# Streaming attention heads: own key tile and preceding block in place of a split window and a separate sink product

## The chip, the cores and the metric

The kernel runs on one core of a Trainium2 chip. The core has TensorE (PE in the profile, with its weight loads as PEld), VectorE (DVE), ScalarE (ACT), GpSimd (POOL) and SyncE (SP), which run their own instruction streams and meet at semaphores. The metric is the time of one execution on the device in microseconds (us). The kernel before takes 270.92 us, the median of three runs from 270.86 to 271.66.

## What is computed

Attention over 4 batches, 8 heads, 768 positions and a head size of 64, then a gated feed-forward layer on the 3072 x 512 result. Heads 0, 2 and 6 are retrieval heads and see all earlier positions. Heads 1, 3, 4, 5 and 7 are streaming heads: a query sees the first 4 positions (the sinks) and the last 64 (the window).

```python
rel = pos[:, None] - pos[None, :]
causal = rel >= 0
stream_keep = causal & ((pos[None, :] < 4) | (rel < 64))
scores = where(causal if retrieval[h] else stream_keep, q @ k.T / 8, -1e9)
x = softmax(scores) @ v                       # heads joined: 3072 x 512
g, val = x @ w_gate, x @ w_val                # 512 -> 1536
ffn = (gelu(g) * val) @ w_out                 # 1536 -> 512
out = x + sigmoid(x @ w_res) * ffn
```

## The kernel before

The work is cut into 24 query tiles of 128 rows, four to a chunk, six chunks (chunk 0 does its attention in two halves of two tiles). Heads go in pairs: (0,2), (4,6), (1,3), (5,7). Python builds a graph of tasks with priorities, and a scheduler orders each engine's tasks; `HINTS` replaces the priorities of single tasks by number. It lets the attention of the next chunk run between the feed-forward matmuls of the current one. All matrices are float16, PSUM is float32.

PE's array is used in four ways, and the scheduler knows them as modes: whole (128 rows x 128 columns), "row" (two halves of 64 rows, for the scores of two heads at once), "col" (two halves of 64 output rows) and "quarter" (four groups of 32 output rows).

For a streaming head, keys lie transposed in `qkt` (features in partitions). A query tile of 128 is scored in two halves of 64 queries, each against the 128 keys that end where it ends:

```python
# scores(), line 857, mode "row"; kt is None for a streaming head
parts = [(max(0, q0 * 128 - 64 + 64 * s), q0 * 128 + 64 * s, 64, o + 64 * s) for s in range(2)]
...
e.matmul(at(scr)[:, oo:oo + w], lhsT=side(BB, low, 1)[half, k0:k0 + 128],
         rhs=side(BB, low, 0)[half, qq:qq + w], start=True, stop=True)
```

The exp (ACT, line 873) moves them to SBUF, and a mask is multiplied on (DVE, line 909). Then the weights times values, with v and a copy `vs` of v that is shifted by 64 rows. Each half of 64 queries is a matmul on half of the array, two at a time:

```python
# weigh() / windows(), line 981, mode "col"; 0.03 us planned for each pair
for s in range(2):
    val = at(BB.v)[:, i, h, :] if s or i == 0 else at(BB.vs)[:, i - 1, h, :]
    r.append(e.matmul(at(av)[64 * s:64 * s + 64, o:o + 65],
                      lhsT=at(P.et)[:, w + 64 * s:w + 64 * s + 64], rhs=val, ...))
```

The sinks are a product of their own. One block a chunk (two in chunk 0) scores all five streaming heads against 32 keys on quarters of the array, one exp follows (`ek`), and each head and tile with a preceding tile adds one whole-array matmul with `vk`, a tile that is zero but for the sink rows:

```python
# sink_scores(), line 948, mode "quarter"
e.matmul(at(scr)[32 * j:32 * j + 32, o:o + w_], lhsT=at(BB.qkt)[half, 1, p, 0:32], rhs=..., ...)
# sinkf(), line 1005, whole array
e.matmul(at(av)[:, o:o + 65], lhsT=at(sinks.et)[:, ko:ko + 128], rhs=at(batch(b).vk)[:, sl, :], ...)
```

Retrieval heads take one whole-array matmul for each key tile (line 991). The other lines that the prediction names: 679 transposes q and k for chunks 0 and 1, 694 empties these to `qkt`; 1116 (and 1098 for halves of chunk 0) are the gate and value matmuls, 1128 the gelu; 1146 is the residual gate, 1161 the second feed-forward product; 1178 are matmuls on a blank tile that keep PE busy until the first gate matmul; 603 fills `vk`, 622 copies to `vs` in chunk 0.

```python
# PSUM banks by kind: (how many at once, which)
"sc": (2, [(2, 3), (4, 5)]), "gv": (4, one(6, 7, 5, 4, 3, 2)), "av2": (1, [(0, 1)]), "out": (2, one(6, 7))
```

Of the kernel before, what the change touches and what calls it, by code (L numbers as in the profile page):

```python
# [4 lines left out]
NHEAD = 8  # L5
SEQ = 768
# [36 lines left out]
VK = ((1, 4), (3, 4), (4, 5), (4, 7))  # L43
# [3 lines left out]
    "0:-96.05 3:-32.5 13:-14.98 398:-205.14 399:-3161.01 400:-242.48 401:-60.67 406:194.11 428:585.68 "  # L47
    "430:523.84 442:461.16 444:1172.07 587:-105.78 592:-108.69 613:396.07 617:407.42 620:-11.7 640:556.2 "
    "642:106.88 643:194.09 646:-2979.21 649:-102.44 659:511.02 686:-2.88 687:77.5 695:496.52 696:499.45 "
    "698:-3129.77 703:60.14 704:-184.95 705:-133.38 707:183.02 708:380.49 711:7.46 712:149.85 713:-50.64 "  # L50
    "715:-14.97 722:1121.95 725:480.98 726:449.69 731:-39.24 732:60.67 733:-318.24 737:-43.72 738:419.39 "
    "739:143.85 743:67.93 744:-230.75 746:-318.2 749:428.99 755:137.07 756:5.66 757:60.69 761:-9.34 "
    "762:495.92 764:2489.99 778:1098.32 789:2479.4 791:2501.2 807:953.41 837:1156.8 842:1419.06 877:2567.99 "
    "879:1563.79 880:2429.98 883:2507.13 898:1013.73 933:1964.55 937:1029.47 939:1471.24 940:2476.14 "
    "955:3421 962:3506.26 963:3575.25 971:3584.03 984:2490.73 989:3565.66 1020:3589.17 1022:2520.47 "
    "1036:2494.69 1066:3486.98 1103:3422.44 1109:3530.5 1114:4315.61 1115:4410.02 1124:-926.78 1134:4596.47 "
    "1141:3465.41 1143:2510.98 1146:2495.35 1152:4653.43 1157:112.2 1170:3039.97 1193:107.93 1248:3488.54 "
    "1265:3479.95 1266:4395.47 1271:4430.01 1272:4484.04 1275:-26.92 1284:5420.01 1289:3472.11 1290:4444.38 "
    "1293:-34.14 1295:3453.61 1302:4490.78 1305:3510.02 1316:3998.02 1318:3550.85 1319:3550.87 1320:4107.35 "
    "1349:3529.55 1351:5429.99 1355:3583.42 1414:5485.04 1451:1066.16 1462:4552.31 1474:4473.03 1475:6343.89 "  # L60
    "1480:4497.31 1530:6505.9 1534:2349.36 1556:5501.98 1602:6498.99 1637:6513.87 1670:7448.62 1687:7406.44 "
    "1689:5504.27 "
# [120 lines left out]
VK_AT = -18.5  # L183
VS_DMA = 0
# [277 lines left out]
def build_kernel(nc, q, k, v, w_gate, w_val, w_out, w_res, out):  # L462
# [7 lines left out]
    m_win = sb("m_win", [128, 7, 128], FP16)  # L470
# [9 lines left out]
    P_vs = Pool(many("vs", 2, [128, NT - 1, NHEAD, DHEAD + 1], FP16))  # L480
    P_vk = Pool(many("vk", 2, [128, 8, DHEAD + 1], FP16))
    P_qkt = Pool(many("qkt", 2, [128, 2, NPAIR, SEQ], FP16))
    P_q6 = Pool(many("q6", 2, [128, 2, SEQ], FP16))
    P_er = Pool(many("er", 2, [128, 4608], FP16))
    P_es = Pool(many("es", 2, [128, 1024], FP16))
    P_ek = Pool(many("ek", 1, [128, 640], FP16))
# [29 lines left out]
    def chain(prio, fns):  # L516
        prev = None
        for n, fn in fns:
            prev = G.add("pool", c_pool(n), fn, [prev], prio, name="const")
        return prev  # L520

    def spread(on, prio, dst, src, n, dep):
        return G.flex({e: (0.15 + 0.0003 * n if e == "dve" else 0.45, lambda e_, e=e: (
            e_.activation(out=dst, in_=src, func=AF.Copy) if e == "act" else e_.tensor_copy(out=dst, in_=src)))
            for e in on}, [dep], prio, name="spread")
# [5 lines left out]
    t_causal = chain(-54, [(128, lambda e: e.memset(m_causal[:, :], 1.0)),  # L531
                           (128, aff(m_causal[:, :], ALU.is_ge, 0.0, 0, [[1, 128]], -1))])


    t_win = chain(-53, [
        (256, lambda e: e.memset(m_win[:, 1:3, :], 1.0)),
        (256, aff(m_win[:, 1:3, :], ALU.is_ge, 0.0, -1, [[0, 2], [0, 2], [-1, 64]], 1)),
        (256, aff(m_win[:, 1:3, :], ALU.is_ge, 0.0, WINDOW, [[0, 2], [0, 2], [1, 64]], -1)),

        (64, aff(m_win[:, 2, 64:128], ALU.is_ge, 1.0, -N_SINK, [[0, 64]], 1)),  # L540
        (64, lambda e: e.memset(m_win[:, 2, 0:64], 1.0)),
        (64, aff(m_win[:, 2, 0:64], ALU.is_ge, 0.0, 0, [[1, 64]], -1))])
    t_win0 = [spread(("dve",), -50, m_win[:, 3:5, :], m_win[:, 1:2, :].to_broadcast([128, 2, 128]), 256, t_win)]

    t_win = t_win0 + [spread(("dve",), 600, m_win[:, 5:7, :], m_win[:, 1:2, :].to_broadcast([128, 2, 128]), 256, t_win),
                      spread(("dve",), 600, m_win[:, 0, :], m_win[:, 1, :], 128, t_win)]
    for i, vk in enumerate(P_vk.items):
        P_vk.last[i] = [G.add("dve", 0.5, (lambda vk=vk: lambda e: e.memset(vk[:, :, :], 0.0))(), [t_blank], -94, name="vzero")]
# [31 lines left out]
    def batch(b):  # L580
        if b not in batches:
            B_ = B()
            B_.v, B_.vs, B_.vk, B_.qkt = Buf(P_v), Buf(P_vs), Buf(P_vk), Buf(P_qkt)
            B_.vtok, B_.vstok, B_.qtok, B_.ktok = {}, {}, {}, {}

            B_.q6, B_.q6tok = None, {}
            batches[b] = B_
        return batches[b]

    def values(b, a, z, base, each, on_engines=False):  # L590
# [6 lines left out]
        if a == 0:  # L597

            def vk(on, j, h0, h1):
                def fn(e):  # L600
                    o = at(BB.vk)[32 * j:32 * j + N_SINK, 2 * j:2 * j + 2, :]
                    i_ = at(BB.v)[0:N_SINK, 0, h0:h1 + 1:h1 - h0, :]
                    return e.activation(out=o, in_=i_, func=AF.Copy) if on == "act" else e.tensor_copy(out=o, in_=i_)
                return fn
            BB.vktok = [G.flex({"dve": (0.3, vk("dve", j, *hs)), "act": (0.35, vk("act", j, *hs))},
                               [BB.vtok[0]], base + 1500, bufs=[BB.v, BB.vk], name="vk") for j, hs in enumerate(VK)]
            for t in BB.vktok:
                t.slack = 12.0 if b else 0.0
                if b == 0:

                    t.eng, t.alts, t.prio = "pool", None, VK_AT
                    t.dur, t.deps = 0.3, t.deps + [x for x in G.tasks if x.name == "const"]
        a_ = max(a, 1)
        if on_engines:
            ts = []
            for lo, hi, pr in ((1, 2, -75),) + (() if VS_DMA else ((2, 4, 130),)):
                for dst, src, off in ((0, 64, 1), (64, 0, 0)):
                    def vs(on, dst=dst, src=src, off=off, lo=lo, hi=hi):
                        def fn(e):
                            o = at(BB.vs)[dst:dst + 64, lo - 1:hi - 1, :, :].rearrange("p i h d -> p (i h d)")  # L620
                            i_ = at(BB.v)[src:src + 64, lo - off:hi - off, :, :].rearrange("p i h d -> p (i h d)")
                            return e.activation(out=o, in_=i_, func=AF.Copy) if on == "act" else e.tensor_copy(out=o, in_=i_)
                        return fn
                    n_ = (hi - lo) * 520
                    ts.append(G.flex({"dve": (c_dve(n_, 2.4, False), vs("dve")), "act": (c_act(n_), vs("act"))},
                                     [BB.vtok[i - off] for i in range(lo, hi)], pr, bufs=[BB.v, BB.vs], name="vs"))
# [651 lines left out]
```

The softmax here doesn't subtract the row's maximum and nothing guards it: scores larger than these inputs give would overflow.

## Time and profile before

| | us |
|---|---|
| time, median of three | 270.92 |
| span of the profiled execution | 268.8 |
| DVE busy / ACT busy / POOL busy | 140.1 / 139.9 / 87.3 |
| gate and value matmuls of 512 columns (line 1116, two groups) | 74.3 + 74.1 |
| second feed-forward product (line 1161) | 70.4 |
| scores (line 857, biggest group) | 16.9 |
| sink products (line 1005), 100 matmuls | 6.6 |
| window products (line 981), 240 matmuls in four groups | 5.7 + 5.5 + 2.1 + 2.0 |

The granted TensorE clock is 1.000 throughout. A busy time of PE counts each matmul from its start to its modelled end, merged where they overlap, so mean durations (379 ns for 512 columns) are longer than the distance between starts. The page also has a chain of work that ended last, waits by engine, a timeline of instructions and busy times in chosen windows; the lines that carry the reading stand in the prediction.

### The profile page before, as it was taken

To read this page: it belongs to the slowest core of one execution; us is meant where nothing else is said; L and a number is where in the kernel's file an instruction comes from. 1 tells how busy PE (TensorE), PEld (TensorE's weight loads), DVE (VectorE), ACT (ScalarE), POOL (GpSimd) and SP (SyncE) were. 2 spreads that over 40 slices of the span, in tenths; PEclk is the share of its full clock that TensorE was granted. 3 is DMA by queue.
4 is the path that set the end of the run, shared out by engine and by line. 5 is a ranking of instruction groups with operands and counts; after the bars stand their busy time and mean duration, and the time that the engine had idled before them with its cause. 6 is when DMAs were issued, how large, how long until landed. Compare 5 with 4: busy or idle time off the path is not lost.

```text
span 268.8 us, 5676 instructions
## 1 busy us (share of the span) xinstructions
PE 264.2 (98%) x2391; PEld 138.7 (52%) x2391; DVE 140.1 (52%) x273; ACT 139.9 (52%) x215; POOL 87.3 (32%) x124
## 2 busy tenths in 40 slices
PE   8999999999999999999999999999999999999995
PEld 7677465465444455444455444555444455444444
DVE  2698245485264376445476433486145367534344
ACT  3785358783334877136792243984233788233310
POOL 8999508995808029894000000000000000000000
DMA  6999999999999999999994100022000113200013
GB/s 86 171 205 207 185 180 228 169 168 187 171 129 187 154 160 185 216 189 125 184 148 134 41 0 0 2 41 96 25 0 0 39 41 80 78 2 0 1 39 120
DMA packets 97562, 29.38 MB, mean 109 GB/s; under 512 B 85504, under 2 KB 93952, under 8 KB 97536
## 3 DMA queue, kind: packets, MB, share of 16 engines
q0 software_dynamic: 70320, 14.69, 65.5%
q1 hardware_dynamic: 27216, 14.33, 27.9%
q8 instruction: 19, 0.31, 0.5%
q14 instruction: 7, 0.06, 0.1%
HBM read 29.36 MB, written 6.29 MB: 133 GB/s over the span
## 4 chain that ended last, share of the span: by engine, by line
PE 93%; DMA 3%; POOL 1%; DVE 1%; issue 0%; POOLq 0%; DVEq 0%
PE ps L1116 44%; PE ps L1161 23%; PE ps L1146 8%; PE ps L857 5%; PE ps L991 3%; DMA va<-in_v_dram 3%; PE ps L1098 3%; PE ps L981 2%; PE ps L1005 2%; PE ps L1070 1%; POOL qks L555 1%; PE ps L948 1%; PE ps L679 1%; PE ps L1178 1%; DVE otile L1168 0%; DVE otile L1165 0%
## 5 line engine op out<-in xcount | busy, mean ns | idle before, releaser
L1130 DVE SCALAR_TENSOR_TENSOR hT<-gact,ps 128x512 f16<-128x512 f16 x68 | 45.8, 686 | 67.4 <-ACT gact L1128 36.6
L1128 ACT ACTIVATE gact<-ps 128x512 f16<-128x512 f32 x68 | 40.1, 597 | 74.0 <-PE ps L1116 72.5
L1116 PE MATMUL ps<-xT,wv 128*128 128x512 f16 x272 | 74.3, 379 | 0.0
L1116 PE MATMUL ps<-xT,wg 128*128 128x512 f16 x272 | 74.1, 379 | 0.0
L1161 PE MATMUL ps<-wo,hT 128*128 128x512 f16 (+2 forms) x312 | 70.4, 363 | 0.0
L1116 PEld LDWEIGHTS ps<-xT,wg 128*128 128x128 f16 x272 | 26.3, 98 | 31.5 <-ACT xT L1077 0.6
L1116 PEld LDWEIGHTS ps<-xT,wv 128*128 128x128 f16 x272 | 26.2, 98 | 30.5 <-DVE hT L1130 0.5
L1161 PEld LDWEIGHTS ps<-wo,hT 128*128 128x128 f16 x312 | 27.5, 98 | 27.0 <-issue 0.7
L873 ACT ACTIVATE er<-ps 128x1024 f16<-128x1024 f32 (+4 forms) x40 | 34.2, 891 | 9.5 <-PE ps L857 9.4
L555 POOL DMA_DIRECT2D qks<-in_k_dram x36 | 28.3, 827 | 32.4 <-DMA qkt<-qks 21.9
L555 POOL DMA_DIRECT2D qks<-in_q_dram x36 | 28.8, 840 | 0.8 <-POOLq L1260 0.8
L1165 DVE SCALAR_TENSOR_TENSOR otile<-srs,ps 128x512 f32<-128x512 f32 (+2 forms) x26 | 16.8, 644 | 16.5 <-PE ps L1161 16.4
L1146 PE MATMUL ps<-wr,xT 128*128 128x512 f16 x96 | 24.7, 379 | 0.0
L555 POOL DMA_DIRECT2D va<-in_v_dram x24 | 21.6, 926 | 2.7 <-PE ps L1005 2.7
L1149 ACT ACTIVATE srs<-ps 128x512 f32<-128x512 f32 x24 | 14.3, 597 | 15.6 <-PE ps L1146 15.3
L1048 DVE TENSOR_TENSOR xtok<-ps,rcp 128x512 f32<-128x512 f32 (+1 forms) x28 | 16.9, 609 | 0.6
L1168 DVE TENSOR_TENSOR otile<-otile,xtok 128x512 f32<-128x512 f32 (+2 forms) x26 | 16.8, 647 | 0.7
L857 PE MATMUL ps<-qkt 64*128 64x64 f16 (+4 forms) x391 | 16.9, 213 | 0.0
L857 PEld LDWEIGHTS ps<-qkt 64*128 64x128 f16 x391 | 9.8, 94 | 9.4 <-issue 3.4
L873 ACT ACTIVATE es<-ps 128x1024 f16<-128x1024 f32 (+1 forms) x14 | 12.6, 898 | 2.9 <-PE ps L857 2.6
L1146 PEld LDWEIGHTS ps<-wr,xT 128*128 128x128 f16 x96 | 8.7, 98 | 10.0 <-issue 0.7
L1178 PE MATMUL ps<-blank 128*128 128x128 f16 x116 | 11.4, 249 | 1.1 <-DVE blank L527 1.1
(70 smaller groups left out, 212.5 us busy)
## 6 DMA issues: line engine op xcount, KB each, us to landing
out_dram<-otile SPq DMA_DIRECT2D x23, 256.0 KB, 2.2
va<-in_v_dram POOLq DMA_DIRECT2D x24, 128.0 KB, 17.0
qks<-in_k_dram POOLq DMA_DIRECT2D x32, 64.0 KB, 11.9
qks<-in_q_dram POOLq DMA_DIRECT2D x32, 64.0 KB, 12.4
wg<-in_moe_w_gate_dram POOLq DMA_DIRECT2D x3, 512.0 KB, 10.3
wv<-in_moe_w_val_dram POOLq DMA_DIRECT2D x3, 512.0 KB, 10.6
wo<-in_moe_w_out_dram POOLq DMA_DIRECT2D x4, 384.0 KB, 22.2
vs<-va SPq DMA_DIRECT2D x4, 260.0 KB, 7.4
```

Of the source, the lines that this page charges most:

```text
L555: return G.add(eng, issue, lambda e: e.dma_start(out_ap(), in_ap), deps, prio, bufs=bufs, dma=cost, name=name, grp=grp)
L857: return [e.matmul(at(scr)[:, oo:oo + w], lhsT=side(BB, low, 1)[half, k0:k0 + 128], rhs=side(BB, low, 0)[half, qq:qq + w], start=True, sto ...
L873: return e.activation(out=o, in_=i_, func=AF.Exp, scale=SM_SCALE)
L1048: t2 = G.add("dve", c_dve(2 * n * 64), lambda e: e.tensor_tensor(out=xview(), in0=avv(0, DHEAD), in1=scale(), op=ALU.mult), [t1] + xdeps, ...
L1116: return lambda e: [e.matmul(at(dst)[:, :], lhsT=w[:, ci, f * 128:(f + 1) * 128], rhs=at(xtbuf)[:, ci, :], start=(ci == 0), stop=(ci == NC ...
L1128: ta = G.add("act", c_act(512), (lambda gb=gb, ga=ga: lambda e: e.activation(out=at(ga)[:, :], in_=at(gb)[:, :], func=AF.Gelu))(), [tg], p ...
L1130: th = G.add("dve", c_dve(512), (lambda vb=vb, ga=ga, f=f: lambda e: e.scalar_tensor_tensor(out=at(h)[:, f, :], in0=at(ga)[:, :], scalar=0 ...
L1146: e.matmul(at(rb)[:, :], lhsT=at(xtbuf)[:, ci, s], rhs=wr[:, ci, :], start=(ci == 0), stop=(ci == NCB - 1))
L1149: ta = G.add("act", c_act(512), (lambda rb=rb, sr=sr: lambda e: e.activation(out=at(sr)[:, :], in_=at(rb)[:, :], func=AF.Tanh, scale=0.5)) ...
L1161: e.matmul(at(fb)[:, w], lhsT=at(h)[:, fi, s], rhs=wo[:, fi, w], start=(fi == 0), stop=(fi == NF - 1))
L1165: t1 = G.add("dve", c_dve(n), (lambda fb=fb, sr=sr, ot=ot, w=w: lambda e: e.scalar_tensor_tensor(out=at(ot)[:, w], in0=at(sr)[:, w], scala ...
L1168: t2 = G.add("dve", c_dve(n), (lambda ot=ot, lt=lt, w=w: lambda e: e.tensor_tensor(out=at(ot)[:, w], in0=at(ot)[:, w], in1=at(xbuf)[:, lt, ...
```

## The change

Each streaming head now handles a query tile as a retrieval head would: the tile against its own 128 keys, one 128-column score matmul and one whole-array product. The keys before it come in as a second block: the 64 keys that precede the tile, followed by the 4 sinks. For this, keys get a row of 144 columns a tile (`KW`), whose columns 128 to 131 hold copies of the sink keys, so that 64 + 4 keys lie next to each other; `vs` holds the matching 64 + 4 rows of v. The separate sink scores, their exp and products, and the split window products go, and with them the modes "col" (for windows) and "quarter".

```diff
-    parts = [(max(0, q0 * 128 - 64 + 64 * s), q0 * 128 + 64 * s, 64, o + 64 * s) for s in range(2)]
+    deps += [BB.ktok[p, q0], BB.ktok[p, q0 - 1], BB.sktok[p]]
+    parts = [((q0 - 1) * KW + 64, q0, nq, o)]
...
-                mine = [[(b, i if retr[x] else None, i, 1) for b, i in tiles]]
+                mine = [[(b, i, i, 1) for b, i in tiles]]
+                if not retr[x]:
+                    near = [(b, None, i, 1) for b, i in tiles if i]
+                    own = sorted(mine[0], key=lambda y: y[2] > 0)
+                    mine = [own, near] if len(tiles) == 4 else [near + own if len(near) == 1 else own + near]
...
-        sinks = sink_scores(c, [t for t in tiles if t[1] > 0], base + 40 + 5, ek, 256 if l0 else 0)
...
+                    w = P.where[x, i, b, i]
+                    r.append(e.matmul(at(av)[:, o:o + 65], lhsT=at(P.et)[:, w:w + 128], rhs=at(BB.v)[:, i, h, :],
+                                      start=lt == 0 and (n == 4 or x == near[0]), stop=(i == 0), skip_group_check=True))
+                    if i:
+                        w, rows = P.where[x, None, b, i], slice(0, 64 + N_SINK)
+                        r.append(e.matmul(at(av)[:, o:o + 65], lhsT=at(P.et)[rows, w:w + 128], rhs=at(BB.vs)[rows, i - 1, (h - 1) * 65:h * 65],
+                                          start=False, stop=True, skip_group_check=True))
...
-            win.mode = "col"
```

`vs` now needs 64 shifted rows and 4 sink rows, by copies of engines in chunk 0 and by DMA later; the sink keys are copied once for each batch (`sink_keys`, on DVE or ACT). The masks are built anew: three kinds (the own tile where it is the first of a batch and holds the sinks, the own tile elsewhere, the preceding block) from memsets on DVE and eight `affine_select` on GpSimd; a second mask multiplication is made for the preceding blocks. Chunk 1 transposes q and k in separate tasks. `qkt` is split into a buffer of q and one of k.

The task numbers change with all this, so the whole string of `HINTS` is new: 128 priorities are replaced by 203, and the new ones also reach into the first loads (task numbers 385 to 515), which the old ones hardly touched.

## The prediction

> **What bounds the kernel now.** I read the page first: the share of busy time by engine, then the waits of TensorE (PE), then the timeline of PE alone, because a busy PE in this profile need not be a PE at its peak.
>
> ```profile
> PE 264.2 (98%) x2391; PEld 138.7 (52%) x2391; DVE 140.1 (52%) x273; ACT 139.9 (52%) x215; POOL 87.3 (32%) x124
> ```
>
> The waits of PE over the whole span are three, 1.7 us in all, and the last of them ends at 13.33 us:
>
> ```profile
> PE ps L1178 <- DVE blank L527: 1.1, 1, 1.1
> PE ps L991 <- DMA va<-in_v_dram: 0.4, 1, 0.4
> PE ps L679 <- DMA qks<-in_q_dram: 0.2, 1, 0.2
> ```
>
> Up to 19.43 us PE fills its time with matmuls on a blank tile (line 1178, 116 of them). From the first gate matmul at 19.43 us on there are none, and PE waits for nobody. So the span is a start of 19.4 us, then PE's own instruction stream, then a tail of 2.9 us behind the last matmul (which ends at 265.9 us). In the middle part an engine other than PE costs nothing unless it makes PE wait, and each 0.1 us that PE's stream loses or gains is 0.1 us of the result.
>
> So the unit of this prediction is the distance from one start to the next in PE's timeline. Lines of it (start us, us until the modelled end, instruction, count) around one sink-score block and one window block:
>
> ```profile
> 126.33 1.46 PE L1116 MATMUL ps<-xT,wv 128*128 128x512 f16 x6
> 127.71 0.45 PE L948 MATMUL ps<-qkt 64*32 64x384 f16 x12
> 128.10 0.41 PE L857 MATMUL ps<-qkt 64*128 64x64 f16 x16
> 128.44 1.04 PE L1116 MATMUL ps<-xT,wv 128*128 128x512 f16 x4
> ...
> 140.67 0.77 PE L991 MATMUL ps<-va,er 128*128 128x65 f16 x20
> 141.28 2.32 PE L1161 MATMUL ps<-wo,hT 128*128 128x512 f16 x10
> 143.53 0.22 PE L981 MATMUL ps<-va,es 128*64 128x65 f16 x2
> ...
> 143.78 0.19 PE L981 MATMUL ps<-vs,es 128*64 128x65 f16 x1
> 143.91 0.35 PE L1005 MATMUL ps<-vk,ek 128*128 128x65 f16 x6
> 144.09 1.03 PE L1146 MATMUL ps<-wr,xT 128*128 128x512 f16 x4
> ```
>
> Three things are to be seen. A 512-column matmul takes 0.216 us, so ten from 141.28 end at 143.44, but the window block (array split by columns) starts at 143.53: a change of the array's split costs about **0.095 us**. Leaving it costs the same: the last window starts at 143.78, its slot is some 0.03, the next matmul starts at 143.91. A whole-array matmul of 65 columns takes **30 ns** (20 in 0.61 us on line 991, six in 0.18 us on line 1005). And a window block of 16 half-array matmuls, two at a time, takes 0.38 us with its exit, where eight whole-array ones would take 0.24.
>
> **What the Trainium skill says.** "TensorE: Matmul & The Clock Gate", section "Back-to-back issue gap", gives N/2.4 + 2.5 ns between warm matmuls: 29.6 ns for 65 columns and 55.8 for 128. The trace agrees for 65 (30 ns); for 128 I use the page's figure as an estimate. "TensorEngine Tiling (Array Packing)", section "Key Properties", says that a change of tiling mode drains TensorE; the trace agrees, with 0.095 us at each change. The first page's section "LDWEIGHTS (loading the stationary operand)" says that a load's time depends on its columns and not on its rows, so the new 68-row load should cost what a 128-row one does; here 64-row loads of 128 columns take 94 ns and 128-row ones 98, and both lie under other matmuls. The second page's section "PSUM Bottleneck" warns that packing doesn't speed up the emptying of PSUM; that is one rival below.
>
> **What goes.** I summed start-to-start distances from 19.4 us on, by line. Line 981 (220 half-array window matmuls) has 5.69 us, line 1005 (some 95 sink products) 3.15, line 948 (five sink-score blocks, quarters of the array) 1.92: 10.76 us with the exits. The entries stand in the line before. Ten window blocks and five sink-score blocks are entered from a whole-array line, 15 x 0.095 = 1.4 us; but three of these are followed by a score block (two rows of the array), which then needs an entry of its own, 0.3 us back. Removed: 10.76 + 1.4 - 0.3 = **11.9 us**.
>
> **What comes on PE.** Five heads stream (1, 3, 4, 5, 7). Chunks 1 to 5 have 20 query tiles, 17 of them with a preceding tile, and the second half of chunk 0 has two and two. Each own tile is one matmul and each preceding block one: 5 x (20 + 17 + 2 + 2) = 205 whole-array matmuls x 30.2 ns = **6.2 us**, with no change of split.
>
> Scores: the own tile takes one 128-column matmul where two of 64 stood (55.8 against 2 x 29.2 ns, -0.1 us over all). The preceding block is new, 128 columns for each tile. Pairs (1,3) and (5,7) run it in both row halves at once: 17 x 2 x 55.8 ns = 1.9 us. Head 4 shares its pair with retrieval head 6, and its 17 x 55.8 = 0.95 us lies partly beside that head's blocks; I take 0.6. Together **+2.4 us**. Chunk 0's scores lie before 19.4 us.
>
> More score blocks: a score task fills one of two groups of two PSUM banks, with up to four query tiles in each bank. Counting banks by the code, chunks 1 to 5 go from 9+10+7+9+10 = 45 tasks to 11+13+10+11+13 = 58. The trace has about 30 score blocks for the 45, 1.5 tasks each. At that rate 13 more tasks make 9 more blocks; if they all join existing ones, none. I choose 5, each with an entry and an exit: **+1.0 us**. Chunk 1's q and k transposes are split in two, say one block more: **+0.2 us**.
>
> Sum: -11.9 + 6.2 + 2.4 + 1.0 + 0.2 = **-2.1 us**.
>
> **The start.** Taken off: 1.54 us of GpSimd copies (line 603) that stand ahead of a weight load, 1.04 us of memsets on VectorE while it is idle, two short exps of the sink scores (0.44 us in the first half). Put on: exps of the streaming pairs from 512 to 768 columns (0.60 to 0.81 us) and masks from 0.41 to about 0.55 in the first half, to 1024 columns in the second, three small copies of sink keys. ScalarE and VectorE are both nearly full from 10 to 19 us, and the additions about cancel the removals. The order of the loads and tasks is new too, and its effect can't be read from this profile. I take 0, give or take 1 us.
>
> So 270.9 - 2.1 = **268.8 us**.
>
> **Rivals.** *ScalarE takes over.* Scores and exps may only run between the last gelu of a chunk and the table load for the next. In chunk 5 this stretch shows:
>
> ```profile
> core 0: us, PE busy (x) PEld busy (x) DVE busy (x) ACT busy (x) POOL busy (x), PEclk, DMA share, GB/s
> 210.00:231.00 21.00, 21.00 (x262) 11.04 (x262) 13.15 (x25) 15.21 (x20) 0.00 (x0) 1.00 0.18 52
> ```
>
> ```profile
> ACT er L873 <- PE ps L857: 2.3, 4, 0.9
> ACT ek L955 <- PE ps L948: 0.9, 1, 0.9
> ```
>
> The second fence holds ScalarE's waits for scores in 205 to 233 us: 3.2 us. The change adds two exps of 1024 columns (1.02 us each), about 0.6 for head 4, and drops the sink exp (0.70): +1.9 us. That fits into 3.2 us, but barely; DVE gets some 1.8 us of masks on 13.2 of 21. If it doesn't fit in all five chunks, PE waits 0.5 us or so in each and the gain is gone: about 271. *The score blocks eat the gain.* If each of the 13 tasks opens its own block, +2.6 in place of +1.0: about 270.4. *The new order does more than the change.* PE has no waits after 13 us, so order can only win fewer changes of split (87 after 19.4 us, 0.095 us each; halving would be 4 us) or an earlier first gate matmul: 265 to 267. A bad order could lose as much. *A transfer is late*: fewer rows are copied on chip (64 and 4 in place of two times 64), and PE waits for no load after 13.33 us; I give it little.
>
> **Range and chances.** The parts that I chose (head 4's share, five blocks, the start) carry about 2 us either way together, the order another 2: 265.8 to 271.8. Faster by over 2% means below 265.5, which needs the order to bring 3 us beyond the sum; slower by over 2% means above 276.3, which needs PE to wait in every chunk.
>
> **What would show it.** In the changed kernel: no half- or quarter-array products of streaming heads; about 205 whole-array ones after the start at 30 ns; 34 to 39 score blocks; PE waits still under 2 us; first gate matmul between 18.4 and 20.4 us. PE waits on exps or masks would prove the first rival, a first gate matmul away from 19.4 us or far fewer changes of split the third.

## The result, and the profile after

The changed kernel takes **275.56 us** (median of four runs, 274.34 to 276.38), the one before in the same comparison 270.89 us (270.57 to 271.66). The ratio is **1.016**, 95% interval 1.0125 to 1.0195: slower by 4.7 us, where the prediction had 2.1 us of gain and a range that ended at 271.8.

The page's first line (busy time by engine) answers to the one shown of before:

```profile
PE 265.3 (97%) x2215; PEld 141.3 (52%) x2215; DVE 148.8 (55%) x291; ACT 145.6 (53%) x221; POOL 86.0 (32%) x120
```

TensorE has 176 instructions less and is busy 1.1 us longer; VectorE carries 8.7 us more, ScalarE 5.7. Busy time alone doesn't tell where 3.8 us of span (268.8 to 272.6) come from. The waits of TensorE do better (line and tile waited for, total us, times, longest):

```profile
PE ps L1068 <- DMA wv<-in_moe_w_val_dram: 1.7, 1, 1.7
PE ps L1130 <- DVE blank L532: 1.2, 1, 1.2
PE ps L1068 <- DVE xT L1029: 0.6, 1, 0.6
...
PE ps L1068 <- DMA wg<-in_moe_w_gate_dram: 0.2, 1, 0.2
```

Before, the last wait ended at 13.33 us. Now TensorE waits behind the first gate matmul as well, 3.1 us in all: 1.9 for gate and value weights, 0.8 in the last chunk (0.6 here, and 0.2 for `x`), the rest in two waits of 0.2. TensorE's timeline (start us, us until the modelled end, instruction, count, idle before it and what ended that) shows the place of the first two:

```profile
20.88 0.60 PE L1050 MATMUL ps<-xT,wg 128*128 128x256 f16 x4
...
25.42 1.46 PE L1068 MATMUL ps<-xT,wg 128*128 128x512 f16 x6
28.60 1.04 PE L1068 MATMUL ps<-xT,wv 128*128 128x512 f16 x4 [1.72 <-DMA wv<-in_moe_w_val_dram]
...
31.16 1.04 PE L1068 MATMUL ps<-xT,wg 128*128 128x512 f16 x4 [0.22 <-DMA wg<-in_moe_w_gate_dram]
```

The span falls into three parts, as in the prediction: up to the first gate matmul, from there to the start of TensorE's last row of matmuls, and the tail.

| profiled execution, us | before | after | difference |
|---|---|---|---|
| first gate matmul | 19.43 | 20.88 | +1.45 |
| from there to the last row of PE (263.07, 266.92) | 243.64 | 246.04 | +2.40 |
| tail | 5.7 | 5.7 | 0 |
| idle time before starts that waited, middle part | 0 | 3.1 | +3.1 |
| delay of these starts | 0 | 3.9 | +3.9 |
| middle part without the delay | 243.6 | 242.1 | -1.5 |

The delay is longer than the idle time, because a wait is counted from the modelled end of the matmul before it. After a 512-column matmul the next start comes 0.216 us later when nothing is waited for, but the modelled end lies 0.38 us behind the start, so 0.16 us of each such wait is not seen as idle. I worked the delay out from start to start: the distance in front of each of the six waits, less the usual distance for that pair (2.10 - 0.22 us in front of 28.60).

So the change does save 1.5 us in TensorE's stream, and 1.45 us of start and 3.9 us of delay stand against it. These make 3.8 us of span. The other 0.9 us of the 4.7 lie between executions: the profiled one is the fastest of the four of after, two of the others show a mean granted clock of 0.994, and the fourth is 1.0 us longer at full clock.

Why is the start later? In both kernels the second load of v lands at 13.3 us (13.29 and 13.24), and from there to the first gate matmul TensorE has no wait. The busy times of that stretch, before and after (stretch, its length, PE, PEld, DVE, ACT, POOL with counts, clock, DMA share, GB/s):

```profile
13.33:19.43 6.10, 6.10 (x125) 4.47 (x126) 5.58 (x20) 4.90 (x13) 6.04 (x9) 1.00 1.25 204
13.29:20.88 7.59, 7.59 (x149) 6.42 (x150) 7.13 (x24) 6.42 (x11) 7.59 (x11) 1.00 1.20 181
```

TensorE's own work in it is about the same (4.1 and 4.0 us from start to start), but its order holds 59 blank matmuls instead of 25, 3.6 us instead of 1.95, and these make the difference. VectorE works 1.55 us longer, so blanks may stand where TensorE would have to wait for it anyway. Which of the two it is, the last experiments test.

Why do the weights come late? GpSimd issues the loads. Here is its timeline before:

```profile
5.01 0.91 POOL L555 DMA_DIRECT2D va<-in_v_dram  x1
...
10.24 0.78 POOL L555 DMA_DIRECT2D wg<-in_moe_w_gate_dram  x1
```

and after:

```profile
6.47 0.90 POOL L564 DMA_DIRECT2D va<-in_v_dram  x1
...
10.53 0.77 POOL L564 DMA_DIRECT2D wg<-in_moe_w_gate_dram  x1
...
12.74 0.78 POOL L564 DMA_DIRECT2D wo<-in_moe_w_out_dram  x1
```

Two things differ. The loads of v start 1.5 us later, because mask steps stand between the loads of q and k; and a slab of the output weights (`wo`) is issued ahead of the last three of the six gate and value slabs. From issue and the median time to landing, the second value slab lands at 24.6 us before and at 28.6 after, while TensorE, done with 6 matmuls from 25.42 us, would have used it at 26.72. Already the first gate slab lands late (16.9 before, 18.8 after), though it is issued only 0.3 us later. The busy times from 10 to 19 us (columns as above) show that the transfers moved less in that time, first before, then after:

```profile
10.00:19.00 9.00, 8.60 (x170) 6.02 (x170) 7.69 (x27) 7.63 (x17) 8.83 (x16) 1.00 1.61 187
```

```profile
10.00:19.00 9.00, 8.88 (x167) 6.73 (x162) 8.29 (x25) 7.36 (x13) 9.00 (x12) 1.00 1.53 158
```

187 GB/s against 158. The gap lies between 11 and 17 us (184 GB/s against 149); up to 11 us the rates are 149 and 145, and the last of the four loads of v lands at 15.2 and 15.1 us. So it is the weights behind the loads of v that lose time. Why the rate falls there, the trace does not tell; the experiments below show which edits bring it back.

### The profile page after: what moved, and what is told of

Its sections match the earlier page's. It is cut to its first block, busy times and chain, and to the rows that moved or that the text cites. A ratio compares the mean times of both kernels' runs of the same rounds, so it can differ in the third digit from the quotient of the medians.

```text
span 272.6 us, 5348 instructions
## 1 busy us (share of the span) xinstructions
PE 265.3 (97%) x2215; PEld 141.3 (52%) x2215; DVE 148.8 (55%) x291; ACT 145.6 (53%) x221; POOL 86.0 (32%) x120
## 3 DMA queue, kind: packets, MB, share of 16 engines
q1 hardware_dynamic: 28164, 13.12, 24.9%
## 4 chain that ended last, share of the span: by engine, by line
PE 76%; DMA 9%; SPq 6%; POOL 4%; DVE 3%; issue 1%; POOLq 0%; DVEq 0%
PE ps L1068 35%; PE ps L1113 21%; PE ps L1098 7%; DMA wg<-in_moe_w_gate_dram 6%; SPq L735 5%; PE ps L874 5%; PE ps L960 3%; DMA q<-qt 2%; PE ps L947 1%; POOL va L564 1%; PE ps L951 1%; PE ps L1050 1%; PE ps L678 1%; PE ps L1022 1%; DVE otile L1117 1%
## 5 line engine op out<-in xcount | busy, mean ns | idle before, releaser
L1068 PE MATMUL ps<-xT,wv 128*128 128x512 f16 x272 | 72.1, 379 | 2.3 <-DMA wv<-in_moe_w_val_dram 1.7
L1068 PE MATMUL ps<-xT,wg 128*128 128x512 f16 x272 | 71.6, 379 | 0.2 <-DMA wg<-in_moe_w_gate_dram 0.2
L890 ACT ACTIVATE er<-ps 128x1024 f16<-128x1024 f32 (+4 forms) x41 | 34.9, 884 | 13.0 <-PE ps L874 12.9
L564 POOL DMA_DIRECT2D qks<-in_k_dram x36 | 29.0, 834 | 32.3 <-DMA qt<-qks 16.1
L890 ACT ACTIVATE es<-ps 128x1024 f16<-128x1024 f32 (+1 forms) x24 | 22.4, 950 | 4.6 <-PE ps L874 4.6
L1117 DVE SCALAR_TENSOR_TENSOR otile<-srs,ps 128x512 f32<-128x512 f32 (+2 forms) x26 | 16.8, 645 | 12.8 <-PE ps L1113 12.3
L1101 ACT ACTIVATE srs<-ps 128x512 f32<-128x512 f32 x24 | 14.4, 599 | 12.4 <-PE ps L1098 11.8
L874 PE MATMUL ps<-qt,kt 64*128 64x128 f16 (+3 forms) x371 | 20.3, 230 | 0.0
L1120 DVE TENSOR_TENSOR otile<-otile,xtok 128x512 f32<-128x512 f32 (+2 forms) x26 | 16.8, 647 | 0.7
L874 PEld LDWEIGHTS ps<-qt,kt 64*128 64x128 f16 x371 | 11.7, 94 | 10.0 <-issue 3.4
L925 DVE TENSOR_TENSOR es<-es,m_win 128x1024 f16<-128x1024 f16 (+1 forms) x24 | 14.9, 637 | 2.6 <-ACT es L890 2.4
L1130 PE MATMUL ps<-blank 128*128 128x128 f16 x156 | 13.9, 245 | 1.2 <-DVE blank L532 1.2
## 6 DMA issues: line engine op xcount, KB each, us to landing
wv<-in_moe_w_val_dram POOLq DMA_DIRECT2D x3, 512.0 KB, 15.1
```

Source lines behind the costliest of these rows:

```text
L564: return G.add(eng, issue, lambda e: e.dma_start(out_ap(), in_ap), deps, prio, bufs=bufs, dma=cost, name=name, grp=grp)
L874: return [e.matmul(at(scr)[:, oo:oo + w * 128], lhsT=keys(BB, low)[half, k0:k0 + 128], rhs=side(BB, low, 0)[half, qq:qq + w, 0:128], start ...
L890: return e.activation(out=o, in_=i_, func=AF.Exp, scale=SM_SCALE)
L925: tm = G.add("dve", c_dve(w * L, 1.8 if L == 2 else 1.5, False), (lambda view=view, m_=m_: lambda e: e.tensor_tensor(out=view(), in0=view( ...
L1068: return lambda e: [e.matmul(at(dst)[:, :], lhsT=w[:, ci, f * 128:(f + 1) * 128], rhs=at(xtbuf)[:, ci, :], start=(ci == 0), stop=(ci == NC ...
L1117: t1 = G.add("dve", c_dve(n), (lambda fb=fb, sr=sr, ot=ot, w=w: lambda e: e.scalar_tensor_tensor(out=at(ot)[:, w], in0=at(sr)[:, w], scala ...
```

## Experiments

All edits act on the graph behind or ahead of `G.schedule()`. Where one moves tasks in an engine's list, the waits are worked out anew for the new order.

### The order, and the structure without it

With the list `HINTS` empty, both kernels run in the scheduler's default order.

```diff
-    for x in "".join(HINTS).split():
+    for x in ():
```

For the kernel after:

> The changed kernel without its list of single priorities, so that every task has the default priority and the loads go in the default order; the computation is the same. With the next kernel it separates the structure from the order. If the order alone is at fault, this is within 1.5 us of the kernel before without its list; if the structure costs time, it is 3 us or more slower than that. Both will be slower than 275 us, as the lists were made to take waits out.

For the kernel before:

> The kernel before without its list of single priorities. Partner of the run above: order alone at fault means the two are within 1.5 us; structure at fault means this one is 3 us or more faster.

Before: 279.67 us (1.033 of the tuned before, 1.031 to 1.035). After: 283.89 us (1.047, 1.0438 to 1.0504). So both orders had been tuned, by 8.8 and 8.3 us, and without them the new structure is still 4.2 us behind. The start is 0.84 us later (20.12 to 20.96), TensorE's waits behind the first gate matmul grow from 4.7 to 7.3 us, none of them for weights, and after lost clock (0.988 in three of four executions, 1.000 in all of before). In the trace the clock is at half for 6.8 us from 239.9 us on, next to waits of 0.46 and 1.56 us, which is up to 3.4 of the 4.2 us. So the tuned order alone isn't the culprit: in this other order, too, the structure comes with a later start and more waits. Where they end differs with the order, so the tuned kernel's own waits have to be tested one by one.

### The weight slab ahead

`wo_later` moves the first output slab of after behind the last gate and value slab:

```diff
     span = G.schedule()
+    for line in (G.prog["pool"], G.order_):
+        t = next(t for t in line if t.seq == 391)              # first slab of wo
+        line.remove(t)
+        line.insert(next(n for n, u in enumerate(line) if u.seq == 385) + 1, t)
```

> The changed kernel with one load moved and nothing else: the first slab of the output weights, which GpSimd issues ahead of the last three gate and value slabs, is issued behind them. Theory 1 (order of the loads): the PE waits on the value slab (1.7 us) and the gate slab (0.2 us) fall to under 0.5 us in all, and the time falls from 275.6 by about 2 us to 273.5. Theory 2 (the new structure itself makes the stream of PE longer): the time stays within 0.5 us of 275.6, because the wait comes back elsewhere.

275.49 us, ratio 1.0159 (1.0119 to 1.02): nothing gained. The second value slab landed at 28.2 us instead of 28.6, TensorE still waited 1.2 us for it, and another wait grew, in chunk 2, for an on-chip copy of q (0.23 us in after):

```profile
92.75 0.33 PE L874 MATMUL ps<-q 64*128 64x384 f16 x1 [1.49 <-DMA q<-qt]
```

So the slab ahead isn't enough to explain the late weights; moving it alone saves 0.3 us of landing. The longer wait for q is only in small part time won earlier: TensorE came there 0.25 us sooner than in after, and the copy, issued 0.1 us later, took 7.25 us to land instead of 6.36.

`before_wo_early` makes the opposite test, an output slab moved ahead of three gate and value slabs in the kernel before (the same edit, task 386 ahead of 382).

> The kernel before with one load moved and nothing else: the first slab of the output weights is issued ahead of the last three gate and value slabs, as in the changed kernel. Theory 1: PE, which waits for no weights now, waits 1 to 2 us for them between 24 and 32 us, and the time rises from 270.9 to about 272.5. Theory 2: no change beyond 0.5 us.

272.68 us, ratio 1.0075 (1.0045 to 1.0104). TensorE waits 1.94 us for gate weights at 28.86. The windows around it (columns as above) show a second price:

```profile
26.00:28.00 2.00, 0.92 (x6) 0.23 (x4) 0.07 (x1) 0.87 (x2) 2.00 (x4) 1.00 1.24 206
28.00:30.00 2.00, 1.14 (x5) 0.56 (x6) 0.00 (x0) 0.00 (x0) 2.00 (x3) 0.92 1.25 204
30.00:32.00 2.00, 2.00 (x8) 0.99 (x7) 0.00 (x0) 0.86 (x2) 0.41 (x1) 0.50 1.75 182
32.00:34.00 2.00, 2.00 (x8) 0.77 (x7) 0.69 (x1) 0.72 (x2) 0.00 (x0) 0.73 1.82 181
34.00:36.00 2.00, 2.00 (x13) 1.12 (x12) 0.74 (x2) 0.50 (x1) 0.00 (x0) 1.00 1.87 178
```

The third number from the right is TensorE's granted clock. It is 1.00 during the wait, then 0.92, 0.50 and 0.73, and 8 matmuls run in 2 us instead of 13. The clock that is missing, 2 x (0.08 + 0.50 + 0.27), is 1.7 us, or 3.4 us at half speed. Against a span of 272 us that is a mean clock of 0.994, the very number of two executions of after; these were not traced, so that they lost it in the same way is not shown. It happened in one of the four executions of `before_wo_early` (span 272.1 us, the others 270.3 to 271.0). A wait of nearly 2 us can thus cost its own length and 1.7 us more; the traced execution of after, with waits of 1.72 and 0.22 us, kept its clock.

### Orders found anew

I let the order be searched again for both kernels, with the loads assumed to land later than the planner had them (0.4 to 2 us more, by kind).

```diff
-HINTS = ( ... 203 priorities ... )
+HINTS = ( ... priorities found under the later landings ... )
+    for t in G.tasks:
+        if t.dma and t.name == "ld" and not 393 <= t.seq <= 400:
+            t.late += 0.4 if t.seq < 384 else 2.0 if t.seq < 393 else 1.0
+        if t.dma and t.name in ("q6", "dT", "vs"):
+            t.late += 0.7
```

> The changed kernel, same computation, with its order planned anew under the assumption that loads land later than it now assumes (weights by 2 us, other loads by 1, copies on the chip by 0.7). Theory 1 (the loss is the order of the loads and the clock that falls after the waits): no wait of PE for a weight or a row over 0.3 us, clock 1.000 in all runs, and the time is 272.0 or less, at least 3 us below the changed kernel's 275.6. Theory 2 (the structure costs the time): the waits for loads go, but the start stays at 20.9 us and waits on exps, masks and norms appear, and the time stays at 274 or above.

> The kernel before, its order planned anew in the same way and with the same assumption. It is the fair partner of the run above. Theory 1: within 1 us of it, so that structure alone is worth nothing much either way. Theory 2: 3 us or more faster than it.

`replan_after`: 273.52 us, ratio 1.0088 (1.0061 to 1.0116), no wait for weights, full clock in all executions. That lies between the two theories (272.0 or less, 274 or more). The first gate matmul comes at 21.56 us and the middle takes 244.32, or 242.4 without the delay by its waits. `replan_before`: 279.59 us, ratio 1.0309 (1.0268 to 1.0351): one wait of 3.86 us at 94.91 us for a copy of q, and a clock of 0.987 to 0.994. It is no fair partner for the other; it shows how much one bad order can cost with the structure unchanged.

### What holds the start: loads of q and k, or blanks

On top of `replan_after`, `loads_first` puts the four loads of q and k first on GpSimd; `loads_first_half_blanks` also leaves out every second blank matmul behind the first 42; `before_half_blanks` leaves these out of the kernel before.

```diff
     span = G.schedule()
+    for line in (G.prog["pool"], G.order_):
+        first = [t for t in line if t.seq in (393, 394, 395, 396)]
+        line[:] = first + [t for t in line if t.seq not in (393, 394, 395, 396)]
...
+    warm = [t for t in G.prog["pe"] if t.name == "warm"]
+    gone = set(warm[42::2])
+    for line in (G.prog["pe"], G.order_):
+        line[:] = [t for t in line if t not in gone]
```

> The newly planned changed kernel (replan_after) with one thing moved: GpSimd issues the first four loads of q and k ahead of the steps that build the masks, which stand between them now. If the start is set by these loads: the wait of PE for q (0.8 us at 7.9 us) goes, the first gate matmul comes at 20.8 us in place of 21.6, and the time falls by 0.7 to 272.8. If the start is set by the exps and copies on ScalarE and VectorE, the first gate matmul stays within 0.3 us of 21.6.

> The run above, and every second matmul on the blank tile after the first 42 left out. The blank matmuls are part of PE's fixed order, so they may hold the start at its planned length. If so, the first gate matmul comes another 0.5 us or more earlier; if ScalarE and VectorE set the start, it doesn't move by more than 0.2 us. If the clock needs the blanks, the granted clock falls below 1.000 and the time rises by 1 us or more.

> The kernel before with every second blank matmul after the first 42 left out, the same cut in the old structure. If blanks hold the start: first gate matmul at 19.0 us or earlier, time 270.3 or less. If not: within 0.3 us of 270.8. If the clock needs them: above 271.8.

`loads_first`: 273.45 us (1.0108, 1.0067 to 1.0149), first gate matmul at 21.26, 0.3 us earlier and nothing in the time; the wait for q went, but waits of 0.62 and 0.59 us for k came. `loads_first_half_blanks`: 274.88 us (1.0151, 1.0111 to 1.019); TensorE idled, and the clock fell to 0.98 to 0.99 in three of four executions. In the traced one it was at half from 12.3 to 19.2 us, so the first gate matmul at 22.35 says nothing about blanks; the one execution at full clock took 274.12 us. `before_half_blanks`: 270.70 us, ratio 0.9998 (0.9989 to 1.0008), first gate matmul at 19.24: blanks don't hold before's start. For after this pair doesn't answer it.

### The loads of v early

The late landings pointed at the mask steps between the first loads. `early_loads` issues q, k and v first and the mask steps between and behind them; `early_loads_wo_later` also has the output slab behind.

```diff
+    new = [394, 393, 2, 396, 395, 397, 13, 398, 6, 399, 7, 400, 8, 9, 10, 11, 12]
+    line = G.prog["pool"]
+    line[:17] = [next(t for t in line[:17] if t.seq == n) for n in new]
+    line = G.prog["dve"]
+    for t in [t for t in line if t.name == "spread"][:2]:
+        line.remove(t)
+        line.insert(next(n for n, u in enumerate(line) if t in u.deps), t)
```

Tasks 393 to 400 are loads of q, k and v, 6 to 13 mask steps; "spread" are the VectorE copies of masks, which now stand just ahead of their first use.

> The kernel after, with the first eight loads of q, k and v issued by GpSimd before most of the mask steps (values begin at about 4.7 us instead of 6.47, the mask steps follow between and behind them, the two VectorE copies of the mask move with them), and with the first slab of the output weights behind the last gate and value slab. Theory A (the weights land late because the loads ahead of them on GpSimd's queue start late, and the output slab then stands ahead of two of them): the first gate slab lands near the 16.9 us of before instead of 18.8, the second value slab near 25 instead of 28.6, TensorE's 1.9 us of waits for gate and value weights vanish, the clock stays at full speed, and the time is 272.5 to 273.5 us, about 2.5 less than after. Theory B (the time is set by the total work ahead of the weights on the queues, and what is won by the early issue stands in the queue anyway): the first gate slab still lands after 18.3, a weight wait of 1 us or more stays, and the time is within 0.7 us of the 275.5 of the run in which only the output slab was moved. The first gate matmul may shift by up to 0.5 us either way, for the masks are ready later.

> The same early loads of q, k and v alone; the first slab of the output weights stays ahead of two of the gate and value slabs. Theory A: the first gate slab near 17 us as in the run beside it, the second value slab about 2 us later than there (the slab that stands ahead), near 27, so about half the waits for weights are left (0 to 1 us), and the time is 273 to 274.5 us. Theory B: waits for weights as in after (1.5 to 2 us) and 275 to 276 us.

`early_loads_wo_later`: 273.49 us (1.0102, 1.008 to 1.0125). `early_loads`: 273.37 us (1.0098, 1.008 to 1.0117). Four executions each within 0.05 us, full clock. The first gate slab lands at 16.8 us in both. TensorE's waits in `early_loads`:

```profile
PE ps L1130 <- DVE blank L532: 1.2, 1, 1.2
PE ps L947 <- DVE er L925: 1.0, 1, 1.0
PE ps L1068 <- DVE xT L1029: 0.6, 1, 0.6
PE ps L874 <- DVE qt L693: 0.4, 1, 0.4
PE ps L947 <- DVE es L925: 0.2, 1, 0.2
PE ps L1022 <- DVE x L998: 0.2, 1, 0.2
```

No weights are left in it, with the output slab ahead or behind. But the first gate matmul is now at 22.52 us, 1.6 us later than in after, so that even a slab landing at 28.6 us would have been waited for only some 0.2 us. It is the landing of the second value slab that tells the causes apart:

| second value slab lands at, us, one execution each | output slab ahead | output slab behind |
|---|---|---|
| loads of v late (after, `wo_later`) | 28.6 | 28.2 |
| loads of v early (`early_loads`, `early_loads_wo_later`) | 27.0 | 24.9 |

The late loads of v cost 1.6 to 3.3 us of landing, as theory A has it, and the slab ahead costs 2.1 more where they are early, little where they are late. The middle takes 243.47 us, what before takes. The whole loss now stands ahead of the first gate matmul, and the new wait for a masked tile (`er`, 1.0 us) says why: the masks are complete at 10.9 us instead of 8.8.

### Fewer mask steps, then fewer blanks

`early_masks` makes the masks in three GpSimd steps and four small VectorE steps and has the output slab behind. `early_masks_no_sinks` leaves out two VectorE copies of sink values (those rows of `vs` stay zero, so three tiles of the first batch lack the sinks' values).

```diff
+    pool_[:17] = [T[n] for n in (394, 393, 2, 396, 395, 397, 13, 8, 398, 6, 399, 400)]   # masks: 13, 8, 6
...
+    small = {7: ([T[6]], lambda e: e.memset(m_win[64:128, 3, :], 1.0)),
+             10: ([T[8], T[13]], lambda e: e.tensor_tensor(out=m_win[:, 5, :], in0=m_win[:, 5, :], in1=L, op=ALU.mult)),
+             11: ([T[10]], lambda e: e.tensor_copy(out=m_win[:, 4, :], in_=m_win[:, 5, :])),
+             12: ([T[11], T[7]], lambda e: e.tensor_copy(out=m_win[0:N_SINK, 4, :], in_=m_causal[0:N_SINK, :]))}
...
+    for n, lo, hi in ((402, 1, 2), (404, 2, 4)):                    # early_masks_no_sinks alone
+        T[n].deps = []
+        T[n].fn = lambda e, lo=lo, hi=hi: e.memset(at(batches[0].vs)[64:64 + N_SINK, lo - 1:hi - 1, 0:455], 0.0)
```

> The kernel after with the early loads of q, k and v and the output slab behind (as in the run with early loads and the output slab moved), but with the masks made in three GpSimd steps instead of eight; the rest of them are four small VectorE steps (a product of two masks, two copies, one fill) put behind its first eviction. Values are issued at 4.8, 6.2, 7.4 and 8.3 us and the masks are whole at about 8.5 us instead of 10.9. Theory A (the start of the two early-load kernels is held by the late masks: TensorE waited 1.1 us for a masked tile at 17.6 us): the first gate matmul comes at 20.0 to 21.0 us instead of 22.5, no wait for weights, full clock, the middle still 243.2 to 243.6 us, and the time 271.0 to 272.3 us, within 1% of before. Theory B (the start is held by something else, the score banks or the work of ScalarE and VectorE): the first gate matmul after 21.5 and 272.7 to 273.5 us.

> The run beside it, and VectorE's two copies of the sink values into the second key block (0.65 and 0.27 us on four partitions in the trace of after, at 12 to 14 us) are left out: those rows are filled with zeros before the first eviction, while VectorE stands idle, so the sinks' values are left out of three tiles of the first batch. If VectorE holds the start (it was busy 11.6 of 14.3 us there), the first gate matmul comes 0.5 to 0.9 us earlier than in the run beside it and the time falls by as much; if the start is held by the score banks or by ScalarE, both stay within 0.2 us.

`early_masks`: 272.58 us (1.0058, 1.0037 to 1.008). The wait for the masked tile is gone, and the start falls from 22.64 to 21.62 us: the late masks had held part of it, though less than theory A had (20.0 to 21.0). `early_masks_no_sinks`: 272.17 us (1.0055, 1.0035 to 1.0075). In its trace the first gate matmul comes at 20.95 us, 0.67 earlier, as forecast if VectorE holds the start. But the executions of each kernel differ by 1.0 us, each start is read from one of them, and the two sets of times overlap, so the cost of the sink copies is not shown.

`early_masks2` replaces the two dear VectorE copies (0.47 and 0.61 us) by two GpSimd steps and one product; `early_masks2_fewer_blanks` also leaves out 38 of the 156 blanks, every second one behind the first 80.

```diff
+    pool_[:17] = [T[n] for n in (394, 393, 2, 396, 395, 397, 13, 8, 398, 9, 10, 399, 6, 400)]   # masks: 13, 8, 9, 10, 6
...
+    T[12].fn = lambda e: e.tensor_tensor(out=m_win[:, 4:6, :], in0=m_win[:, 4:6, :], op=ALU.mult,
+                                         in1=m_causal[:, :].rearrange("p (o q) -> p o q", o=1).to_broadcast([128, 2, 128]))
...
+    warm = [t for t in G.prog["pe"] if t.name == "warm"]            # early_masks2_fewer_blanks alone
+    gone = set(warm[80::2])
```

> As early_masks, but the two dear VectorE copies of its masks (0.47 and 0.61 us at 7.7 to 9.1 us, the second on four partitions) are gone: GpSimd makes two more steps (0.5 us, the weights go out 0.5 us later, at about 9.6) and VectorE multiplies two masks by the causal one in a single step. Theory A (VectorE's mask steps held the start of early_masks): the first gate matmul at 20.3 to 21.2 us instead of 21.6, and 271.2 to 272.2 us. Theory B (TensorE itself, with its blank matmuls at fixed places of the order, holds the start: 156 blanks against 116 in before): within 0.3 us of early_masks, 272.2 to 272.9.

> As the run beside it, with 38 of the 156 blank matmuls (every second one behind the first 80) left out, some 2.1 us of TensorE's time at 0.056 us each before the first gate matmul. In the trace of the run without sink copies the chain from 10.3 us to the first gate matmul is TensorE alone, without a wait. Theory B: the first gate matmul comes 1 to 2 us earlier than in the run beside it, at 19.3 to 20.2 us, with the clock still full, and the time falls to 270 to 271.2 us, level with before. Theory A (the blanks fill time in which the masks, exponentials and evictions hold TensorE anyway, as half the blanks did in before): waits take their place and the time stays within 0.4 us of the run beside it; or the clock falls for lack of work and it is slower.

`early_masks2` takes **272.21 us**, ratio 1.0053 (1.0036 to 1.0069). The first gate matmul is at 21.01 us, about where after has it (20.88), but the second value slab lands near 24.6 us and TensorE doesn't wait for weights. So with the gate at its place, early loads and the slab behind take these waits away. `wo_later`, with the slab behind but late loads of v, had the gate at 21.11 us and still waited 1.2 us: the early loads are needed. The slab behind is worth little here: with the slab ahead it landed at 26.95 us in `early_loads`, and the first use is now at 26.84, so some 0.1 us of wait would be left, an estimate from these two traces. The time overlaps with that of `early_masks`, so what this last change of the masks is worth isn't shown.

The chain that ends in the first gate matmul is TensorE alone from 4.9 us on, without a wait. With fewer blanks the gate comes 0.57 us earlier, at 20.44, not the 1 to 2 us of theory B, and the chain of waits (start us, us, what) now runs over VectorE, and for 1.3 us over ScalarE; its first part:

```profile
10.75 0.69 DVE qt L693
11.44 0.47 DVE es L925
11.91 0.60 DVE kt L693
12.51 0.03 issue
12.54 0.55 DVE vs L621
13.10 0.01 issue
13.11 0.84 DVE vs L621 x2
```

The window of the same kernel says it in one line (PE 5.00 of 6 us, DVE 5.96; with all blanks PE has 6.00 and DVE the same 5.96):

```profile
14.00:20.00 6.00, 5.00 (x90) 3.54 (x85) 5.96 (x21) 5.17 (x8) 6.00 (x8) 1.00 1.24 205
```

Most of the blanks had filled time in which VectorE holds the start; some 0.6 us of the later start were blanks alone. The time is 273.51 us, the median of four of which one took 277.59 at a clock of 0.987; without it the median is 272.88, ratio 1.0088 (1.0056 to 1.012). In the trace the earlier start was lost again at a wait of 1.5 us for a copy of q, which landed 0.6 us later than in `early_masks2`. No version of the changed kernel was faster than the kernel before.

## Why the prediction was wrong

**The method held.** The span is a start, TensorE's stream and a tail, and each 0.1 us of TensorE's idle time is paid. What failed was the assumption that the stream would stay free of waits.

**"PE waits for no load after 13.33 us; I give it little"** is the step that failed worst. It is true of before, where the second value slab lands at 24.6 us. But the diff shows new priorities for the first loads and eight mask steps on the engine that issues them, and that slab had only some 2 us of slack (first used at 26.61 us). The slabs behind it had next to none: the third gate slab lands at 27.14 us and is used at 27.18, the third value slab at 29.68 and 29.79, so before was just in time. In after the second value slab could be used at 26.72 and lands at 28.6. The two waits for weights delay TensorE by 2.3 us (1.9 us of them idle time); that two executions lost their 1.7 us of clock by them is likely, but not traced. With loads early and the output slab behind, the waits vanish and the clock is full: against its own runs of before, `early_masks2` is 1.5 us behind where after is 4.7.

**"The start: 0, give or take 1"** failed too: +1.45 us. I counted ScalarE's and VectorE's work and called it a draw, but VectorE has 11.6 us of work from 5.7 to 20 us where it had 10.7, and the masks are on GpSimd's way. In the trace of after itself TensorE doesn't wait in that stretch; its order holds more blanks. Even with masks and loads early the start is 21.01 us against 19.43. That is +1.58 us, about what `early_masks2` is still behind (1.5 us), for the 1.5 us that its stream saves are taken back by 1.8 us of delay at four waits. With blanks taken out, VectorE's chain ends it at 20.4: of the 1.58 us some 0.6 are blanks, and the other 1.0 stands where the chain runs mainly over VectorE. I did not separate which of VectorE's new steps (wider masks, copies to `vs`) makes up that last microsecond.

**TensorE's stream: -2.1 us predicted**, -1.5 measured: without the delay by waits the middle part takes 242.1 us in after, `early_loads` and `early_masks2` alike, and 243.6 in before. The mechanism was right, and two terms of the sum were too small. What went had 10.77 us (10.76 predicted). The products took 6.6 us for 6.2: 197 of them, for 8 came before the first gate matmul, at 33 ns each, not 30.2. Scores took 2.9 us more in their own line, and whole-array blocks are left for scores 31 times instead of 21, 10 x 0.095 = 0.95 us: 3.9 against my 2.4 + 1.0 + 0.3. Here the base was wrong too: I had "about 30" score blocks in before, and there are 24 from the first gate matmul on; after has 31, seven more where I chose five. Together the two terms are 0.6 us, the difference between 2.1 and 1.5. The 55.8 ns for 128 columns came out (56 ns on line 1022), and so did the weight load of 68 rows (98 ns, as for 128 rows).

**The first rival, ScalarE takes over**, may have come true in the last chunk only, and small. The stretch of its exps lasts 16.8 us in after and in `replan_after` (211.7 to 228.5) where before had 14.4 (210.7 to 225.1), and then TensorE waits for the normalised rows. The lines of after:

```profile
233.75 0.62 PE L1022 MATMUL ps<-ident,x 128*128 128x128 f16 x8 [0.16 <-DVE x L998]
234.98 0.59 PE L1068 MATMUL ps<-xT,wv 128*128 128x512 f16 x2 [0.61 <-DVE xT L1029]
```

That is 0.8 us idle (1.1 us of delay), and it stays in `early_loads` and `early_masks2`. That the longer stretch causes it was not tested: `nohint_before` has the same two waits (0.69 and 0.61 us) without the change. The Trainium skill's "TensorEngine Tiling (Array Packing)", section "PSUM Bottleneck", warns that packing speeds up TensorE but not the emptying of PSUM; here some packing went and TensorE's stream still got shorter, while ScalarE, whose exps empty PSUM, got 5.7 us more work and VectorE 8.7.

**The third rival, the order**, had the right size ("a bad order could lose as much" as 4 us), but I set it beside the change instead of inside it: the order of the first loads and the place of the blanks came with it. Changes of the array's split fell from 88 to 69, 1.8 us at 0.095 each, but that is the structure and not the order: with both lists empty they fall from 96 to 70. The sum had counted it, and it is part of the stream's -1.5.

## What to carry to other kernels

When a kernel has one saturated engine and no waits, list the slack of each transfer that feeds it (landing against first use) before counting instructions: a change that touches the issuing engine in the first microseconds can spend more than the instructions save. Work moved off the saturated engine lands on the others in stretches where they are full (here the start and the last chunk), so cost it by stretch and not over the span. Judge a structural change under more than one order, since waits move with it: each order here had its own.

## What the runs showed of the hardware

A wait of TensorE of 1.94 us was followed, 0.8 us after it resumed (worked out from the windows above), by 3.4 us at half clock, in one of four executions of the same kernel. In the traces of `nohint_after`, `replan_before` and `loads_first_half_blanks` the missing clock, added up in the same way, is 3.4 us, or 6.8 us at half. The Trainium skill's "TensorE: Matmul & The Clock Gate", section "HAM oscillation — how this bites in real kernels", sets the rule at idle gaps longer than about 3.4 us; here a shorter gap was enough, so the measurement decides. That page's Part 1 calls the activity window free-running, which would fit that some executions escape; no run here tests it.

Copies on VectorE over four partitions were no cheaper than over many: 455 columns took 0.27 us on 4 partitions and 0.28 on 64 in `early_masks2`, and 910 columns 0.65 us on 4 (there the source is one block read twice) and 0.40 on 64 in after. The same copy of 455 columns over 64 partitions took 0.63 us in `early_loads`, so one such value alone tells little.
